# A fused attention and two-MLP kernel: another order of ScalarE's and VectorE's work in the first group, a second block of x through TensorE, and a later first load of r and k

## The chip, the cores and the metric

The kernel runs on one core of a Trainium2 chip. The metric is device time in microseconds (us) of one execution. An execution counts as faster or slower here only from about half a per cent on.

## The reference

Three layers follow each other, all in float32.

```
# 1. linear attention with decay: B=2, H=8 heads, S=768 steps, D=48
y[t]  = r[t] . (state + (u*k[t]) v[t]^T)      # per head
state = w[t] * state + k[t] v[t]^T
# 2. x = y with the heads side by side, [2, 768, 384]
xk = mu_k*x + (1-mu_k)*x_prev ;  xr = mu_r*x + (1-mu_r)*x_prev
x  = sigmoid(xr @ w_r) * (relu(xk @ w_k)**2 @ w_v)          # d_ff = 1024
# 3. gated MLP with a product over the sequence
h = gelu(x @ w_in) ; u, v = halves of h ; v = layernorm(v)*g
out = x + (u * (w_sg @ v + b_sg)) @ w_out
```

## The kernel before, in words

**Units.** The 2 x 768 tokens are cut into 4 groups of 384, and each group's 8 heads into 4 pairs: 16 units, numbered 0 to 15, of one pair over 384 tokens (3 chunks of 128). Units 0 to 3 are the first group. A unit's chunks are worked in parallel form: VectorE first makes decayed copies of r and k (`attn_prep`: two scans `pf` and `pr`, a reciprocal between them, then `kp`, `rp`, `ruk`). TensorE then works a unit in four steps:

- S (`attn_sc`): transposes `kp` into PSUM (`kt_ps`), which ScalarE evicts to `kt`; products of `rp` with `kp` (`sc`), which VectorE masks into `am`; column sums of `ruk`, which VectorE multiplies into `vb`.
- K (`attn_kv`): `kt` by v gives each chunk's state addition `kv`; VectorE adds them up into `zt` and `zcar`, and ScalarE writes scaled copies (`sblk`, `scar`) onto block diagonals. For the first group these ScalarE copies are kept in lists and issued later: "soon" (chunks 0 and 1, four copies a unit) and "late" (the last chunk: `zcar` and two `scar` copies).
- Y (`attn_y`): `am` by v and `vb`, into the PSUM tile `y`.
- Z (`attn_z`): adds `rp` by the scaled states; ScalarE evicts `y` to `yo`, and DMAs carry `yo` into `xx`, which holds x transposed: 3 blocks of 128 rows. A pair has 96 rows, so block 0 takes pairs 0 and 1, block 1 pairs 1 and 2, block 2 pairs 2 and 3.

**Order around the change.** TensorE's order is written out by hand: S0 K0 S1 K1 Y0 Z0 S2 K2 Y1 Z1 S3 K3 Y2 Z2 Y3 Z3, then the first tiles of the second layer (`k`, `r`, `v` steps), between which the next group's units are put. `dummy(n)` issues n matmuls whose result nobody reads: 22 at the start, 2 ahead of each S and Y of the first group, 6 ahead of the first `k` step. Between `in_order.__enter__` and `__exit__`, ScalarE and VectorE run compute instructions strictly in the order in which the program text issues them; elsewhere, and on SyncE's queue of DMAs, priorities set by `at(...)` (planned due times) decide. In that fixed order a unit's "soon" copies stood ahead of the next unit's eviction `kt`.

**The join.** The first `k` step needs all three blocks of `xk` (`moe1_prep`: ScalarE writes `mu*x` to `dx`, VectorE adds `(1-mu)*x_prev` into `xkh`). Blocks 0 and 1 are read from `xx` once its DMAs have landed. Block 2 doesn't wait for a DMA: `sel_run` gathers its rows from the `yo` tiles of pairs 2 and 3 by two matmuls with selection matrices (`sel_make`) into a PSUM bank `bs`, from which ScalarE and VectorE read. Weights come as 64-bit words and are cut to float32 by one ScalarE and one VectorE instruction for each tile (`conv_moe1`: `top`, then `wk`, `wr`, `wv`).

**Queues.** `load_t(0)` issues unit 0's r and k (`urk`) from ScalarE's queue, ahead of `actw`, a one-element sigmoid that brings the activation table in; nearly all other loads, and the DMAs out of `yo`, go through SyncE's queue in order.

Of the kernel before, what the change touches and what calls it, by code (L numbers as in the profile page):

```python
# [17 lines left out]
CH = 128  # L18
# [15 lines left out]
SPARE = 2  # L34
ND0 = 22
ND = 2
ND4 = 4
NDK = 4
N_EARLY = 10
# [28 lines left out]
def emit(tc, tin, nin, vt, consts, ucp, pars, b_sg, w_k, w_v, w_r, w_in, w_sgT, w_out, outT):  # L68
# [22 lines left out]
    class at:  # L91
# [7 lines left out]
        def __exit__(self, *a):  # L99
            tc.cur_priority = self.old  # L100

    subs = []
    for g in range(NG):
# [115 lines left out]
    def wide(i):  # L219
        return i >= NP * N_DIAG  # L220

    def load_uvt(i):
        src = tin[subs[i // NP][0] * NP + i % NP]
        for q in rows(i == NP * N_DIAG):
            with at(TS["Y", i] - 9):
                SP.dma_start(uvts[q], src[q, WL + 2 * G:WL + 3 * G])

    def load_t(i):
        s, hp = divmod(i, NP)
        g, c0, n = subs[s]  # L230
        src = tin[g * NP + hp]
        w, rk = uws[i % 3], urks[i % 3]
        e = A if i < 1 else SP
        for q in rows(i < 3):
            with at(TS["S", i] - 9 if i >= 2 else -19.9 + 0.05 * i):
                SP.dma_start(w[q], src[q, 0:WL])
        for q in rows(i < 3):
            with at(TS["S", i] - 8.5 if i >= 2 else -19.8 + 0.1 * i):
                e.dma_start(rk[q], src[q, WL:WL + 2 * G].rearrange("p (q t) -> p q t", q=2))
        if i == NP * N_DIAG:  # L240
            load_uvt(i)
        uw[i], urk[i] = w, rk

    def load_n(i):
        s, hp = divmod(i, NP)
        g, c0, m = subs[s]
        src = nin[g * NP + hp]
        e = SP if i < 2 else A
        v = pa.tile([128, m, PW], F32, name="uv", tag="uv", bufs=4)
        with at(TS["K", i] - 9 if i >= 2 else -19.5 + 0.1 * i):  # L250
            e.dma_start(v, src[:, c0:c0 + m])
        uv[i] = v
# [133 lines left out]
    def attn_prep(i):  # L386
# [14 lines left out]
        with at(tS - L_PREP):  # L401
            V.tensor_tensor_scan(pf[:, 0:n1], w[:, 0:n1], d1f[:, 0:n1], 1.0, ALU.mult, ALU.max)  # L402
            pe = dr[:, 1:1 + n1].rearrange("p (c t) -> p c t", t=CH + 1)[:, :, CH:CH + 1]
            V.reciprocal(pe, pf3[:, :, CH:CH + 1])
            V.tensor_tensor_scan(pr[:, 1:wl][:, ::-1], w[:, 1:wl][:, ::-1], dr[:, 1:wl][:, ::-1], 0.0, ALU.mult, ALU.add)  # L405
        yield
# [64 lines left out]
    def attn_kv(i):  # L471
# [18 lines left out]
        for c in range(nk):  # L490
# [9 lines left out]
            def scaled(c=c, o=o, sb=sb):  # L500
# [3 lines left out]
                with at(tY - 0.5 + (3 if c == nc_ - 1 else 0.2 * c)):  # L504
                    for h in range(2):
                        hs = slice(h * HP, h * HP + D)
                        A.activation(sb[hs, hs], o[hs], AF.Copy, scale=s["pe"][c][hs])  # L507

# [22 lines left out]
    def attn_z(i):  # L531
# [6 lines left out]
        for c in cs:  # L538
            PE.matmul(y3[0:PR, c], s["us"][c], s["rp"][:, c], start=False, stop=(c == cs[-1]), skip_group_check=True)  # L539
        yo = pa.tile([PR, nc_ * CH], F32, name="yo", tag="yo", bufs=2)  # L540
        s["yo"] = yo
# [7 lines left out]
        with at(TE["Z", i] - 0.2):  # L549
            for h in range(2):  # L550
                a = hp * PW + h * D
                e = a + D
                while a < e:
# [4 lines left out]
                    a += n  # L558
        for f in s.pop("late", []) if i < NP - 1 else []:
            f()  # L560
# [24 lines left out]
    m1 = {}  # L585
    head = {}

    def sel_make():
        t = pl["w"].tile([128, G], F32, name="rs", tag="rs", bufs=3)
        sel = [t[0:PR, q * 128:(q + 1) * 128] for q in range(2)]  # L590
        PL.memset(t, 0.0)
        head["sel"] = sel
        A.activation(sel[0][HP:PR, 0:32], ident[HP:PR, HP + 16:PR], AF.Copy)
        A.activation(sel[1][0:D, 32:32 + D], ident[0:D, 0:D], AF.Copy)
        A.activation(sel[1][HP:PR, 32 + D:128], ident[HP:PR, HP:PR], AF.Copy)

    def sel_run(q):
        x = head["bs"][0]
        if q == 0:
            V.memset(x[:, 0:1], 0.0)  # L600
        PE.matmul(x[:, 1:1 + G], head["sel"][q], st[NP - 2 + q]["yo"], start=(q == 0), stop=(q == 1))

    def moe1_prep(s, which, hold=(), mix=None):
# [8 lines left out]
        def one(j):  # L612
            d = pl["w"].tile([128, t1 - t0], F32, name="dx", tag="dx", bufs=2)
            xj = head["bs"][0] if mix is not None and j == KM - 1 else x[:, j]
            with at(dl - 2.5 + 0.5 * j):
# [277 lines left out]
    with at(-19.95):  # L893
        A.activation(actw, actw, AF.Sigmoid)
    load_t(0)
# [33 lines left out]
    for n, key in enumerate(keys[:n_in]):  # L929
        kd, g = key[0], key[1]  # L930
        if kd in "SY" and g < NP:
            dummy(ND)
        if key == ("Z", NP - 1):
            mix = []
            moe1_prep(0, 0, mix=mix)
            mix[0]()
        if key == ("k", 0, 0):
            mix[1]()
            conv_moe1(0, 1)
            dummy(ND)  # L940
            sel_run(0)
            sel_run(1)
            dummy(NDK)
            rest = attn_prep(NP)
            next(rest)
            mix[2]()
            next(rest)
            conv_moe1(1, 2)
            next(rest, None)
            conv_moe1(2, 3)  # L950
            for f in st[NP - 1].pop("late"):
                f()
            head["order"].__exit__()
        run(key)
        if kd == "K" and g == 0 or kd == "Z" and g < NP - 1:
            for f in st[g + (kd == "Z")].pop("soon"):
                f()
        if kd == "K" and g < NP - 2:
            prep(g + 2)
        if key == ("K", NP - 2):  # L960
            load_unit(NP + 1)
        if kd == "S" and g == NP:
            prep(NP + 1)
            conv_moe1(3)
# [97 lines left out]
```

## Time and profile before

| | us |
|---|---|
| median of 3 runs (lowest, highest) | 364.93 (363.58, 365.13) |
| the profiled execution, its own time | 363.64 |
| its span in the trace | 361.6 |
| TensorE (PE) busy | 343.8 |
| VectorE (DVE) busy | 237.3 |
| ScalarE (ACT) busy | 180.5 |

The span leaves out 2.04 us of the profiled execution's time, before the first and behind the last instruction. Busy time is a sum over the whole span; TensorE's idle time lies almost all in the first 40 us and the last 6. In the timelines below, a line gives the start, the duration (of all instructions merged into it, first start to last end), engine, line of the kernel, operation, out<-in, shapes, count, and in brackets the idle time before it and what ended that.

### The profile page before, as it was taken

To read this page: it belongs to the slowest core of one execution; us is meant where nothing else is said; L and a number is where in the kernel's file an instruction comes from. 1 tells how busy PE (TensorE), PEld (TensorE's weight loads), DVE (VectorE), ACT (ScalarE), POOL (GpSimd) and SP (SyncE) were. 2 spreads that over 40 slices of the span, in tenths; PEclk is the share of its full clock that TensorE was granted. 3 is DMA by queue.
4 is the path that set the end of the run, shared out by engine and by line. 5 is a ranking of instruction groups with operands and counts; after the bars stand their busy time and mean duration, and the time that the engine had idled before them with its cause. 6 is when DMAs were issued, how large, how long until landed. Compare 5 with 4: busy or idle time off the path is not lost.

```text
span 361.6 us, 5957 instructions
## 1 busy us (share of the span) xinstructions
PE 343.8 (95%) x2169; PEld 290.4 (80%) x2169; DVE 237.3 (66%) x515; ACT 180.5 (50%) x427; POOL 41.1 (11%) x64
## 2 busy tenths in 40 slices
PE   8888699989999999999999999999999999999993
PEld 3576367657655568988889999999899998999993
DVE  5972599965548897669643955169889960835531
ACT  2236479766347675167744797395571315301100
POOL 2000003021093200000001316100000000000000
PEclk9899699999999999999999999999999999999999
DMA  8944862655800454001101441451332001010012
GB/s 225 293 161 146 213 188 76 216 146 119 234 3 18 114 152 118 19 16 34 35 18 60 127 134 49 120 177 41 84 78 69 0 22 46 22 45 0 0 70 73
DMA packets 23750, 33.97 MB, mean 94 GB/s; under 512 B 3504, under 2 KB 18032, under 8 KB 23712
## 3 DMA queue, kind: packets, MB, share of 16 engines
q1 hardware_dynamic: 21504, 31.02, 30.3%
q10 hardware_dynamic: 2208, 2.48, 2.5%
q8 instruction: 19, 0.31, 0.4%
q14 instruction: 19, 0.16, 0.2%
HBM read 28.77 MB, written 2.36 MB: 86 GB/s over the span
## 4 chain that ended last, share of the span: by engine, by line
PE 74%; DVE 11%; ACT 6%; DMA 5%; issue 2%; ACTq 0%; SPq 0%; DVEq 0%
PE mm L583 36%; PE mn L583 26%; PE y L525 3%; ACT sblk L507 2%; PE y L539 2%; DMA stg<-w_v 2%; DVE pf L402 2%; PE sc L445 1%; DVE am L468 1%; DMA uw<-tin 1%; PE kv L484 1%; DMA xx<-yo 1%; DVE pr L405 1%; PE mm L909 1%; DVE kl L664 1%
## 5 line engine op out<-in xcount | busy, mean ns | idle before, releaser
L583 PE MATMUL mm<-xkh,wk 128*128 128x384 f32 x96 | 34.6, 506 | 0.0
L571 ACT ACTIVATE gah<-gt 128x384 fp32r<-128x384 f32 x16 | 8.4, 526 | 44.2 <-DVE gt L759 44.2
L583 PEld LDWEIGHTS mm<-xkh,wk 128*128 128x128 f32 x96 | 18.1, 195 | 12.3 <-issue 1.6
L616 ACT ACTIVATE dx<-xx,par 128x384 f32<-128x384 f32 x23 | 14.0, 611 | 26.9 <-DMA xx<-yo 24.7
L507 ACT ACTIVATE sblk<-zt,pf 48x48 f32<-48x48 f32 x64 | 21.2, 331 | 9.3 <-DVE zt L494 6.5
L402 DVE TENSOR_TENSOR_SCAN pf<-uw,d1f 112x387 f32<-112x387 f32 x16 | 16.2, 1011 | 11.3 <-ACT sblk L507 5.0
L583 PE MATMUL mm<-kh,wh 128*128 128x384 f32 x64 | 22.1, 345 | 0.0
L664 DVE TENSOR_TENSOR kl<-kr,kh 128x384 fp32r<-128x384 f32 x24 | 15.1, 629 | 10.2 <-ACT kr L663 10.2
L583 PE MATMUL mm<-kh,wvl 128*128 128x384 f32 x64 | 21.6, 337 | 0.0
L583 PE MATMUL mm<-kl,wh 128*128 128x384 f32 x64 | 21.6, 337 | 0.0
L583 PE MATMUL mn<-wsh,vl 128*128 128x384 f32 x60 | 20.0, 334 | 0.0
L583 PE MATMUL mn<-wsh,vh 128*128 128x384 f32 x60 | 20.0, 334 | 0.0
L583 PE MATMUL mn<-wsl,vh 128*128 128x384 f32 x60 | 20.0, 334 | 0.0
L302 POOL TENSOR_TENSOR w2l<-wf,w2h 128x384 fp32r<-128x384 f32 x12 | 12.8, 1077 | 62.9 <-ACT w2h L301 62.9
L649 ACT ACTIVATE kr<-mm 128x384 f32<-128x384 f32 x27 | 13.0, 480 | 11.5 <-PE mm L583 9.6
L525 PE MATMUL y<-am,uv 128*48 128x128 f32 (+1 forms) x192 | 16.5, 288 | 1.9 <-DVE am L468 1.8
L445 PEld LDWEIGHTS sc<-rp,kp 48*128 48x128 f32 x192 | 12.2, 187 | 6.2 <-issue 4.5
L295 ACT ACTIVATE top<-stg 128x384 f16<-128x384 bf16 x21 | 13.0, 640 | 8.4 <-DMA stg<-w_in 3.9
L468 DVE TENSOR_TENSOR am<-sc,cst 128x384 f32<-128x384 f32 x32 | 16.2, 548 | 1.2 <-PE sc L445 1.2
L583 PE MATMUL mm<-kh,wv 128*128 128x384 f32 x48 | 16.3, 490 | 0.0
L445 PE MATMUL sc<-rp,kp 48*128 48x128 f32 x192 | 15.5, 289 | 0.9 <-DVE am L468 0.9
L405 DVE TENSOR_TENSOR_SCAN pr<-uw,d1r 112x387 f32<-112x387 f32 x16 | 16.0, 998 | 0.4
(210 smaller groups left out, 968.6 us busy)
## 6 DMA issues: line engine op xcount, KB each, us to landing
urk<-tin SPq DMA_DIRECT2D x26, 144.0 KB, 3.3
wh<-w_k SPq DMA_DIRECT2D x8, 384.0 KB, 5.1
stg<-w_v SPq DMA_DIRECT2D x8, 384.0 KB, 4.1
stg<-w_in SPq DMA_DIRECT2D x8, 384.0 KB, 3.5
wq<-tin SPq DMA_DIRECT2D x16, 168.0 KB, 2.5
wsf<-w_sgT SPq DMA_DIRECT2D x12, 192.0 KB, 4.1
outT<-ot SPq DMA_DIRECT2D x12, 192.0 KB, 1.9
uv<-nin ACTq DMA_DIRECT2D x14, 144.0 KB, 2.4
```

The costliest lines, as they stand in the source:

```text
L295: A.activation(box(top.bitcast(F16).rearrange("p (f w) -> p f w", w=2)[:, :, 1]), end, AF.Copy)
L302: e.tensor_tensor(lo, full, hi.bitcast(F32), ALU.subtract)
L402: V.tensor_tensor_scan(pf[:, 0:n1], w[:, 0:n1], d1f[:, 0:n1], 1.0, ALU.mult, ALU.max)
L405: V.tensor_tensor_scan(pr[:, 1:wl][:, ::-1], w[:, 1:wl][:, ::-1], dr[:, 1:wl][:, ::-1], 0.0, ALU.mult, ALU.add)
L445: PE.matmul(sc[h][:, c], s["kp"][hs, c], s["rp"][hs, c], start=True, stop=True)
L468: V.tensor_tensor(am[:, h], sc[h], mask, ALU.mult)
L507: A.activation(sb[hs, hs], o[hs], AF.Copy, scale=s["pe"][c][hs])
L525: PE.matmul(y3[hs, c], uv[i][:, c, h * D:PW if h else HP], s["at"][:, h, c], start=(c == 0), stop=False, skip_group_check=True)
L583: PE.matmul(ps, l, r, start=(first and k == 0), stop=(last and k == len(prods) - 1))
L616: A.activation(d, xj[:, 1 + t0:1 + t1], AF.Copy, scale=mu[:, j:j + 1])
L649: m1[s, "ev", f] = A.activation(kr, ps, AF.Relu).ins
L664: V.tensor_tensor(kl, kr, kh.bitcast(F32), ALU.subtract)
```

## The change

In the first group, a unit's "soon" copies are issued after the next unit's S instead of before it, so that ScalarE evicts `kt` first. For unit 3 they go to VectorE (`tensor_scalar`), issued after K3. Unit 2's "late" copies move behind the join. Block 1 of x is gathered by selection matmuls as block 2 was: four selection matrices, four `sel_run` calls, into both `bs` banks, the first one after Z2, and unit 1's `yo` gets a tile of its own to outlive it; block 0 is mixed ahead of Z2. Unit 4's `attn_prep` is cut once more, and its first scan and the reciprocal are issued ahead of the second block's mix, the second scan behind the third's. The dummy matmuls change from 22 to 20 at the start, from 2 to 4 ahead of each S, from 2 to 1 ahead of each Y of the first group, and from 6 to none ahead of the first `k` step. Unit 0's r and k, and the v tiles of units 2 and 3, are issued on ScalarE's queue behind `actw`.

```diff
@@ -32,10 +34,10 @@
 NTOK = B * S
 NW1 = 2 * KF + KM
 SPARE = 2
-ND0 = 22
-ND = 2
+ND0 = 20
+ND = 1
+NDS = 4
 ND4 = 4
-NDK = 4
 N_EARLY = 10
 T_EARLY = 13.0
 D_EARLY = 1.5
@@ -99,6 +101,7 @@
         def __exit__(self, *a):
             tc.cur_priority = self.old
 
+    head = {}
     subs = []
     for g in range(NG):
         c0 = 0
@@ -219,6 +222,9 @@
     def wide(i):
         return i >= NP * N_DIAG
 
+    def after_table(on):
+        return tc.issue_after(head["actw"]) if on else contextlib.nullcontext()
+
     def load_uvt(i):
         src = tin[subs[i // NP][0] * NP + i % NP]
         for q in rows(i == NP * N_DIAG):
@@ -235,7 +241,7 @@
             with at(TS["S", i] - 9 if i >= 2 else -19.9 + 0.05 * i):
                 SP.dma_start(w[q], src[q, 0:WL])
         for q in rows(i < 3):
-            with at(TS["S", i] - 8.5 if i >= 2 else -19.8 + 0.1 * i):
+            with at(TS["S", i] - 8.5 if i >= 2 else -19.8 + 0.1 * i), after_table(i in (0,)):
                 e.dma_start(rk[q], src[q, WL:WL + 2 * G].rearrange("p (q t) -> p q t", q=2))
         if i == NP * N_DIAG:
             load_uvt(i)
@@ -247,7 +253,7 @@
         src = nin[g * NP + hp]
         e = SP if i < 2 else A
         v = pa.tile([128, m, PW], F32, name="uv", tag="uv", bufs=4)
-        with at(TS["K", i] - 9 if i >= 2 else -19.5 + 0.1 * i):
+        with at(TS["K", i] - 9 if i >= 2 else -19.5 + 0.1 * i), after_table(i in (2, 3)):
             e.dma_start(v, src[:, c0:c0 + m])
         uv[i] = v
 
@@ -402,6 +408,8 @@
             V.tensor_tensor_scan(pf[:, 0:n1], w[:, 0:n1], d1f[:, 0:n1], 1.0, ALU.mult, ALU.max)
             pe = dr[:, 1:1 + n1].rearrange("p (c t) -> p c t", t=CH + 1)[:, :, CH:CH + 1]
             V.reciprocal(pe, pf3[:, :, CH:CH + 1])
+        yield
+        with at(tS - L_PREP):
             V.tensor_tensor_scan(pr[:, 1:wl][:, ::-1], w[:, 1:wl][:, ::-1], dr[:, 1:wl][:, ::-1], 0.0, ALU.mult, ALU.add)
         yield
         pr3 = pr[:, 2:2 + n1].rearrange("p (c t) -> p c t", t=CH + 1)
@@ -504,7 +512,10 @@
                 with at(tY - 0.5 + (3 if c == nc_ - 1 else 0.2 * c)):
                     for h in range(2):
                         hs = slice(h * HP, h * HP + D)
-                        A.activation(sb[hs, hs], o[hs], AF.Copy, scale=s["pe"][c][hs])
+                        if i == NP - 1 and c < nc_ - 1:
+                            V.tensor_scalar(sb[hs, hs], o[hs], s["pe"][c][hs], None, ALU.mult)
+                        else:
+                            A.activation(sb[hs, hs], o[hs], AF.Copy, scale=s["pe"][c][hs])
 
             if i < NP:
                 s.setdefault("late" if c == nc_ - 1 else "soon", []).append(scaled)
@@ -537,7 +548,10 @@
         cs = [c for c in range(nc_) if s["us"][c] is not None]
         for c in cs:
             PE.matmul(y3[0:PR, c], s["us"][c], s["rp"][:, c], start=False, stop=(c == cs[-1]), skip_group_check=True)
-        yo = pa.tile([PR, nc_ * CH], F32, name="yo", tag="yo", bufs=2)
+        if i == 1:
+            yo = pl["w"].tile([128, G], F32, name="kl", tag="kl", bufs=KF)[0:PR]
+        else:
+            yo = pa.tile([PR, nc_ * CH], F32, name="yo", tag="yo", bufs=2)
         s["yo"] = yo
         if hp == 0 and g % GB == 0 and c0 == 0:
             PL.memset(xx[g][:, :, 0:1], 0.0)
@@ -556,7 +570,7 @@
                     q = h * HP + a - hp * PW - h * D
                     (A if i == NP - 1 and h else SP).dma_start(xx[g][p:p + n, j, 1 + c0 * CH:1 + (c0 + nc_) * CH], yo[q:q + n])
                     a += n
-        for f in s.pop("late", []) if i < NP - 1 else []:
+        for f in s.pop("late", []) if i < NP - 2 else []:
             f()
         if hp == NP - 1 and c0 + nc_ == CG and g % GB != GB - 1:
             with at(TE["Z", i] + 2):
@@ -583,22 +597,24 @@
             PE.matmul(ps, l, r, start=(first and k == 0), stop=(last and k == len(prods) - 1))
 
     m1 = {}
-    head = {}
 
     def sel_make():
-        t = pl["w"].tile([128, G], F32, name="rs", tag="rs", bufs=3)
-        sel = [t[0:PR, q * 128:(q + 1) * 128] for q in range(2)]
-        PL.memset(t, 0.0)
+        t = [pl["w"].tile([128, G], F32, name="kl", tag="kl", bufs=KF) for _ in range(2)]
+        sel = [t[q // 2][0:PR, q % 2 * 128:q % 2 * 128 + 128] for q in range(4)]
+        for x in t:
+            PL.memset(x, 0.0)
         head["sel"] = sel
-        A.activation(sel[0][HP:PR, 0:32], ident[HP:PR, HP + 16:PR], AF.Copy)
-        A.activation(sel[1][0:D, 32:32 + D], ident[0:D, 0:D], AF.Copy)
-        A.activation(sel[1][HP:PR, 32 + D:128], ident[HP:PR, HP:PR], AF.Copy)
+        for q, rows_, to, fr in ((0, slice(32, D), 0, 32), (0, slice(HP, PR), 16, HP), (1, slice(0, D), 64, 0),
+                                 (1, slice(HP, HP + 16), 112, HP), (2, slice(HP, PR), 0, HP + 16),
+                                 (3, slice(0, D), 32, 0), (3, slice(HP, PR), 80, HP)):
+            n = min(rows_.stop, PR) - rows_.start if q != 2 else 32
+            A.activation(sel[q][rows_, to:to + n], ident[rows_, fr:fr + n], AF.Copy)
+
+    def sel_bank(j):
+        return head["bs"][j % 2]
 
     def sel_run(q):
-        x = head["bs"][0]
-        if q == 0:
-            V.memset(x[:, 0:1], 0.0)
-        PE.matmul(x[:, 1:1 + G], head["sel"][q], st[NP - 2 + q]["yo"], start=(q == 0), stop=(q == 1))
+        PE.matmul(sel_bank(1 + q // 2)[:, 1:1 + G], head["sel"][q], st[1 + (q + 1) // 2]["yo"], start=(q % 2 == 0), stop=(q % 2 == 1))
 
     def moe1_prep(s, which, hold=(), mix=None):
         g, c0, n = subs[s]
@@ -611,7 +627,7 @@
         dl = TS[("k", "r")[which], s, 0] - (4 if s == 0 and which == 0 else 0)
         def one(j):
             d = pl["w"].tile([128, t1 - t0], F32, name="dx", tag="dx", bufs=2)
-            xj = head["bs"][0] if mix is not None and j == KM - 1 else x[:, j]
+            xj = sel_bank(j) if mix is not None and j else x[:, j]
             with at(dl - 2.5 + 0.5 * j):
                 A.activation(d, xj[:, 1 + t0:1 + t1], AF.Copy, scale=mu[:, j:j + 1])
             with at(dl - 2 + 0.5 * j):
@@ -891,7 +907,7 @@
         mmp["q"] = None
 
     with at(-19.95):
-        A.activation(actw, actw, AF.Sigmoid)
+        head["actw"] = A.activation(actw, actw, AF.Sigmoid).ins
     load_t(0)
     load_t(1)
     with at(-19.75):
@@ -929,36 +945,44 @@
     for n, key in enumerate(keys[:n_in]):
         kd, g = key[0], key[1]
         if kd in "SY" and g < NP:
-            dummy(ND)
-        if key == ("Z", NP - 1):
+            dummy(NDS if kd == "S" else ND)
+        if key == ("Z", NP - 2):
             mix = []
             moe1_prep(0, 0, mix=mix)
             mix[0]()
         if key == ("k", 0, 0):
-            mix[1]()
-            conv_moe1(0, 1)
-            dummy(ND)
-            sel_run(0)
-            sel_run(1)
-            dummy(NDK)
             rest = attn_prep(NP)
             next(rest)
+            sel_run(1)
+            sel_run(2)
+            mix[1]()
+            conv_moe1(1, 2)
+            sel_run(3)
             mix[2]()
             next(rest)
-            conv_moe1(1, 2)
+            next(rest)
+            conv_moe1(2, 3)
             next(rest, None)
-            conv_moe1(2, 3)
-            for f in st[NP - 1].pop("late"):
-                f()
+            for i in (NP - 2, NP - 1):
+                for f in st[i].pop("late"):
+                    f()
             head["order"].__exit__()
         run(key)
-        if kd == "K" and g == 0 or kd == "Z" and g < NP - 1:
-            for f in st[g + (kd == "Z")].pop("soon"):
+        if key == ("Z", NP - 2):
+            conv_moe1(0, 1)
+            sel_run(0)
+        if kd == "S" and 0 < g < NP:
+            for f in st[g - 1].pop("soon"):
                 f()
         if kd == "K" and g < NP - 2:
             prep(g + 2)
         if key == ("K", NP - 2):
             load_unit(NP + 1)
+        if key == ("K", NP - 1):
+            for f in st[g].pop("soon"):
+                f()
+            for q in range(2):
+                V.memset(head["bs"][q][:, 0:1], 0.0)
         if kd == "S" and g == NP:
             prep(NP + 1)
             conv_moe1(3)
```

## Rows read from the trace of the kernel before

**Rows 1.** Stretches, TensorE: stretch, its length, busy us (instructions), clock, DMA share, GB/s
```profile
40.31:46.60 6.29, 6.29 (x12) 0.50 0.80 220
46.60:66.00 19.40, 19.40 (x130) 1.00 0.45 127
...
130.00:355.50 225.50, 224.74 (x1373) 1.00 0.22 62
```

**Rows 2.** Timeline of ScalarE, 6 to 48 us
```profile
14.03 1.40 ACT L507 ACTIVATE sblk<-zt,pf 48x48 f32<-48x48 f32 x4 [4.25 <-DVE zt L494]
15.46 0.45 ACT L434 ACTIVATE kt<-kt_ps 128x336 f32<-128x336 f32 x1
...
20.64 0.49 ACT L548 ACTIVATE yo<-y 112x384 f32<-112x384 f32 x1 [4.73 <-PE y L539]
...
37.34 0.60 ACTq L557 DMA_DIRECT2D xx<-yo  x1
38.37 0.61 ACT L616 ACTIVATE dx<-xx,par 128x384 f32<-128x384 f32 x1 [1.05 <-issue]
```

**Rows 3.** Timeline of TensorE, 8 to 50 us
```profile
15.96 0.88 PE L484 MATMUL kv<-uv,kt 128*64 128x48 f32 x12 [0.70 <-ACT kt L434]
...
20.44 0.59 PE L909 MATMUL mm<-d1f 112*128 112x512 bf16 x2
20.87 0.45 PE L423 MATMUL kt_ps<-cst,kp 112*128 112x112 f32 x3
...
23.86 0.55 PE L484 MATMUL kv<-uv,kt 128*64 128x48 f32 x12 [0.92 <-ACT kt L434]
...
26.33 0.69 PE L539 MATMUL y<-rp,sblk 112*112 112x128 f32 x4
...
32.77 0.69 PE L539 MATMUL y<-rp,sblk 112*112 112x128 f32 x4
...
40.31 2.90 PE L601 MATMUL mm<-yo,rs 112*128 112x384 f32 x4 [3.10 <-DVE mm L600]
...
44.71 4.95 PE L583 MATMUL mm<-xkh,wk 128*128 128x384 f32 x12
```

**Rows 4.** Timeline of VectorE, 5 to 71 us
```profile
14.51 0.96 DVE L402 TENSOR_TENSOR_SCAN pf<-uw,d1f 112x387 f32<-112x387 f32 x1
...
18.19 1.01 DVE L468 TENSOR_TENSOR am<-sc,cst 128x384 f32<-128x384 f32 x2
...
21.95 0.96 DVE L402 TENSOR_TENSOR_SCAN pf<-uw,d1f 112x387 f32<-112x387 f32 x1 [1.67 <-ACT scar L507]
...
47.27 0.96 DVE L402 TENSOR_TENSOR_SCAN pf<-uw,d1f 112x387 f32<-112x387 f32 x1
...
64.54 1.01 DVE L468 TENSOR_TENSOR am<-sc,cst 128x384 f32<-128x384 f32 x2
```

**Rows 5.** Timeline of TensorE, the second layer's start
```profile
51.33 4.14 PE L583 MATMUL mm<-xkh,wk 128*128 128x384 f32 x12
...
65.90 0.88 PE L525 MATMUL y<-am,uv 128*48 128x128 f32 x12
```

**Rows 6.** Stretches, VectorE, the same columns
```profile
47.35:65.50 18.15, 17.29 (x34) 1.00 0.45 121
```

**Rows 7.** Timeline of all engines, 0 to 20 us
```profile
0.73 0.43 ACTq L239 DMA_DIRECT2D urk<-tin  x1
...
1.19 1.28 ACT L894 ACT_TABLE_LOAD   x1 [1.19 <-PEq L1054]
...
2.48 0.20 ACT L894 ACTIVATE actw<-actw 1x1 f32<-1x1 f32 x1
...
7.35 0.56 DVE L409 TENSOR_TENSOR kp<-urk,pr 112x384 f32<-112x384 f32 x1
```

**Rows 8.** Timeline of SyncE's DMA issues, 0 to 80 us
```profile
37.96 1.00 SPq L236 DMA_DIRECT2D uw<-tin  x2
```

**Rows 9.** DMA issues of the first 8 us: KB each, median us to landing
```profile
urk<-tin ACTq DMA_DIRECT2D x1, 336.0 KB, 4.7
```

More of the change, by code (lines that the diff above doesn't have):

```diff
@@ L1 @@
+import contextlib
 import concourse.bass as bass
```

## The prediction

> **What bounds the kernel now.** I read the page's share of each engine first, then the stretches, the timelines of the first 70 us, and the waits. The stretches [rows 1] show two regimes. From 46.6 us on TensorE is busy without a gap at the full clock, and again from 130 to 355.5 us (224.74 of 225.5): there only the time at which its stream starts can move the end. Ahead of 46.6 us it isn't the bound. It stands still for 3.10 us ahead of the selection matmuls at 40.31 [rows 3] and then runs 6.29 us at clock 0.50, the 1.2 GHz level [rows 1]. The reader should see there that what ends last is a chain over engines, unit by unit: in unit 1, ScalarE's four "soon" copies stand from 14.03 ahead of the eviction `kt` at 15.46 [rows 2], and TensorE's K1 waits 0.70 us for that eviction; K2 waits 0.92 us in the same way [rows 3]. The delay comes round: `yo` at 20.64 comes late [rows 2], the "late" copies behind it too, and VectorE's scan `pf` of unit 3 waits 1.67 us for them [rows 4]. At the join, block 1's `dx` at 38.37 sits behind a DMA issue on ScalarE's queue and the landing of `xx` [rows 2].
>
> But the second layer's start has a second, nearly full engine: VectorE is busy 17.29 of 18.15 us from 47.35 to 65.50 [rows 6], its mask for unit 5 starts at 64.54 [rows 4] and TensorE takes it up at 65.90 [rows 5], some 0.35 us after it ends. So I follow two clocks, how much earlier TensorE comes to `k`, and how much earlier VectorE comes to the same work, and the smaller of the two counts.
>
> **The first group, unit by unit.** *Eviction first.* In unit 1 K1 can start 0.70 us earlier, at 15.26, when its predecessors on TensorE end. The two more dummies ahead of S1 cost 0.43 us (two dummies, 20.44 to 20.87 [rows 3]), hidden under the wait of S1's products for VectorE's mask. K1 to Z1 in unit 2's rows takes 26.33 - 23.86 = 2.47 us [rows 3], less 0.2 for one dummy fewer; so Z0 starts at about 17.5. The cost of being wrong here: before, unit 1's steps took longer, 15.96 to 20.64 (`yo`, which waits for Z0's end [rows 2]) less 0.69 for Z0: 3.99, so the same steps at that pace would put Z0 1.5 later. From `yo` to the end of the "late" copies goes 21.95 - 20.64 = 1.31 us [rows 2, 4], so they end near 19.5, and `pf` of unit 3 starts as soon as VectorE is free, 1.67 us earlier, at 20.28.
>
> *The period.* VectorE needs 18.19 - 14.51 = 3.68 us for one unit's copies and, from 18.19 to 20.28 (21.95 less its wait), 2.09 for masks and sums: 5.77 a unit [rows 4]. TensorE needs, from dummies to K, 23.86 - 20.44 - 0.92 = 2.50, plus 0.43 for two more dummies; K to Z 2.47 less 0.2; Z at most 0.69, part of it under the next dummies: 5.7 to 5.9. Before, the period was 32.77 - 26.33 = 6.44 [rows 3]. With 5.8, Z2 starts at 17.5 + 2 x 5.8 = 29.1 instead of 32.77.
>
> *To the last yo.* A selection matmul in float32 is two passes of 384 columns; twelve such passes took 4.14 us [rows 5], so one matmul costs 0.69. Z2 0.5 (its tail under what follows), first selection 0.69, one dummy and Y3 1.7 (2.47 less K's 0.55 and a dummy's 0.2 [rows 3]), Z3 0.69: unit 3's `yo` starts at 32.6 or 32.7 and ends at 33.1 (0.49 [rows 2]). Before, its DMA issue followed it at 37.34: 4.2 us earlier. The four copies that move to VectorE cost 0.35 each on ScalarE (1.40 for four [rows 2]); on VectorE I bound them by 0.2 and 0.35 and take 0.25: 1 us, behind sums of unit 3 that end near 28.2 (two of VectorE's periods of 5.77 from 14.51, masks and sums 2.09), so ready at 29.2 against a need at 31.9. If that cover went, Z3 would slip by at most 1.4. Deferring unit 2's "late" copies takes their 0.8 us out from ahead of `dx`; what is late next is TensorE itself.
>
> **The join.** Before, from the issue at 37.34 to the first `k` at 44.71 went 7.4 us. After, three selections behind Z3 (2.1) end at 34.5; block 1's `dx` waits only for the issue of the DMA on ScalarE's own queue (0.60 plus the 0.43 seen behind it [rows 2]), at 34.1; then `dx` 0.61, `xkh` as long, `top` 0.6, the third `dx` 0.6 and its `xkh` 0.6: all three blocks stand at 36.5. The first `k` starts at 34.5, its third part at 36.5, and its second tile ends at 36.5 + 0.69 + 2.07 = 39.3. Before, these twelve passes ended at 44.71 + 4.95 = 49.66 [rows 3]. TensorE is 10.3 us ahead: 4.2 from the group, the rest from the idle 3.1, the low clock and the six dummies. Should the clock still be low there, the twelve passes cost 0.8 more as before (4.95 against 4.14 [rows 3, 5]), and the three selections up to 2.3 (2.90 for two [rows 3], 1.45 each against 0.69).
>
> **VectorE.** Behind the third `xkh` at 36.5 it has unit 4's second scan (1.0) and five instructions of about 0.5 (17.29 / 34 [rows 6]) to unit 5's `pf`: 39.9 to 40.0, where it was 47.27 [rows 4]. Ahead by 7.3. It cannot close more than the 0.86 us of idle in the next 18.15 us [rows 6]: between 7.3 and 8.2 at unit 5's mask, against TensorE's 10.3. I take 7.8, the middle. TensorE will then wait there for about 2.5 us, which it did not before; from there on both run as before, and beyond 130 us nothing but TensorE.
>
> **The start.** The issue of unit 0's r and k moves from 0.73 [rows 7] to behind the table load, which moves up to about 0.75: 0.75 + 1.28 + 0.20 = 2.25. With 4.7 us to landing [rows 9] it is there at 6.95, and `kp` starts at 7.35 [rows 7]: hidden by 0.4. If it lands 6 us after the issue, `kp` is 0.9 late and VectorE, without a break behind it, carries that through; if the scans ahead of it start earlier because the decays no longer share the engines with it, up to 0.5 is won. I take 0 and keep -0.5 to +0.9. The Trainium skill, "ScalarE: Activation LUTs", section *What ACT_TABLE_LOAD costs*, gives about 1283 ns for the load and about 1380 ns more for a drain. Our trace shows the load but no drain: the sigmoid starts at 2.48, 0.01 us behind the load's end [rows 7]. With the drain the issue would be at 3.6 and `kp` 1 us late, an estimate from that page, and the gain 6.8.
>
> At nothing I cost: more selection matrices (ScalarE waits there anyway), two one-column memsets, a tile of its own for one `yo`, v tiles of units 2 and 3 behind the table load (needed from K2 on).
>
> **The sum.** 363.64 (the profiled execution's own time) - 7.8 = 355.8. It lies 1.3 under the median of three runs, 364.93; half of that on top gives 356.5.
>
> **The rivals.**
> *SyncE's queue decides.* The loads of units 5 to 7 and of weights stand behind unit 3's DMAs: unit 5's decays went at 37.96, right behind the issues at 37.34 [rows 2, 8]. They come forward by 4.2, not by 7.8. For it: unit 5's `pf` would want its decays at 40, and from an issue at 33.8 leaves 6 us. Against: 4.7 to landing is usual [rows 9]. Then the gain is 4.2 to 5: 359 to 360.
> *The lead is eaten.* VectorE's order behind the join is planned anew, and waits appear that weren't there; or the eviction at the head of ScalarE's order, which must wait for transposes, holds the copies that Z needs. Against it: the transposes end long before (K1 waits for nothing else [rows 3]). Gain 0 to 1.8: 363.
> *The clock stays low (slower).* One dummy ahead of Y instead of two, and none ahead of `k`: if the granted clock falls to 1.2 GHz at unit 1, as it did in part before, and now stays there up to the first `k`, the 5.8 us of three units grow. K to the end of Z took 20.64 - 15.96 = 4.68 in unit 1 [rows 2, 3] against 26.33 + 0.69 - 23.86 = 3.16 in unit 2, half as much again: 2.9 a unit, 8.7 in three, and 2.3 for three selections: 7.8 - 8.7 - 2.3, so 3 us slower, 367. It decides from the point where more than two units run low. Against it: dummies a unit rise from 4 to 5, and the idle stretch of 3.1 us is gone.
>
> **How the numbers follow.** My forecast has 0.62, with 353 to 359 as its own range (10.3 ahead kept in full at the one end; 0.9 late at the start, the copies' 1.4 and the low clock's 0.8 at the other: 7.8 - 3.1 = 4.7). SyncE's queue has 0.18, the eaten lead 0.12, the low clock 0.08. For 8 in 10 the range goes from 353 to 361. Half a per cent is 1.8 us, about what can be told from no change: faster 0.82, the same 0.10, slower 0.08.
>
> **What would show it.** Right: `kt` of unit 1 on ScalarE at 12.7, ahead of the copies; `pf` of unit 3 at 20.3 without a wait; Z2 near 29; four selections between 29 and 35; the first `k` near 34.5; clock 1.00 through 34 to 47; a wait of some 2 us of TensorE for VectorE's mask about unit 5's Y. Wrong: a wait of `kp` for its load at the start, unit 5's `pf` waiting for a DMA, a clock of 0.50 behind 16 us, or a first `k` later than 38.

## The result, and the profile after

| | before | after |
|---|---|---|
| median (lowest, highest), us | 364.37 (363.58, 365.13) | 353.24 (352.92, 353.79) |
| the profiled execution, us | 363.64 | 353.79 |
| its span, us | 361.6 | 351.7 |
| TensorE (PE) busy, us | 343.8 | 340.8 |

Four executions of each; the ratio is 0.9696, with a 95% interval of 0.9668 to 0.9724. The medians differ by 11.1 us, the profiled executions by 9.85: before's lay 0.73 us under its median, the changed kernel's 0.55 over its own.

The stretches of all engines after (stretch, length, then busy us and instructions of PE, PEld, DVE, ACT and POOL, granted clock, DMA share, GB/s) stand beside those of [rows 1]. The reader should see the clock column: 1.00 throughout, where before had 0.50 at the join. From 9.0 to 28.9 us TensorE has no gap.

```profile
9.00:28.90 19.90, 19.90 (x233) 15.55 (x231) 18.19 (x43) 8.42 (x25) 0.41 (x1) 1.00 0.81 249
28.90:34.00 5.10, 5.10 (x42) 3.58 (x41) 2.59 (x8) 2.06 (x5) 0.00 (x0) 1.00 0.66 159
34.00:38.40 4.40, 4.30 (x13) 2.08 (x12) 3.83 (x7) 4.34 (x13) 0.33 (x1) 1.00 0.86 248
38.40:56.00 17.60, 17.40 (x123) 11.88 (x121) 16.97 (x33) 14.88 (x34) 2.65 (x2) 1.00 0.65 174
```

ScalarE's timeline after answers to [rows 2]: `kt` stands ahead of the four copies in unit 1, and unit 3's `yo` and its DMA issue come 4.1 us earlier (33.22 for 37.34).

```profile
13.76 0.45 ACT L442 ACTIVATE kt<-kt_ps 128x336 f32<-128x336 f32 x1 [2.91 <-PE kt_ps L431]
14.23 1.40 ACT L518 ACTIVATE sblk<-zt,pf 48x48 f32<-48x48 f32 x4
...
32.70 0.49 ACT L562 ACTIVATE yo<-y 112x384 f32<-112x384 f32 x1 [2.12 <-PE y L550]
33.22 0.60 ACTq L571 DMA_DIRECT2D xx<-yo  x1
33.92 0.58 ACT L632 ACTIVATE dx<-mm,par 128x384 f32<-128x384 f32 x1 [0.73 <-PE mm L617]
```

TensorE's timeline after, beside [rows 3, 5]: S0 at 9.90 (8.84 before), K1 without a wait, Z0 and Z2, the join without a gap, unit 5's Y, and two new waits at unit 5's Z.

```profile
9.90 0.45 PE L431 MATMUL kt_ps<-cst,kp 112*128 112x112 f32 x3
...
15.28 0.55 PE L492 MATMUL kv<-uv,kt 128*64 128x48 f32 x12
...
17.53 0.69 PE L550 MATMUL y<-rp,sblk 112*112 112x128 f32 x4
...
28.84 0.69 PE L550 MATMUL y<-rp,sblk 112*112 112x128 f32 x4
...
32.44 2.10 PE L617 MATMUL mm<-yo,kl 112*128 112x384 f32 x6
34.38 4.67 PE L597 MATMUL mm<-xkh,wk 128*128 128x384 f32 x12
38.89 0.45 PE L431 MATMUL kt_ps<-cst,kp 112*128 112x112 f32 x3
...
55.74 1.21 PE L536 MATMUL y<-am,uv 128*64 128x128 f32 x11 [0.20 <-DVE am L476]
...
60.47 0.47 PE L550 MATMUL y<-rp,sblk 112*112 112x128 f32 x2 [0.40 <-ACT sblk L518]
61.50 0.47 PE L550 MATMUL y<-rp,sblk 112*112 112x128 f32 x2 [0.56 <-ACT sblk L518]
61.81 0.45 PE L431 MATMUL kt_ps<-cst,kp 112*128 112x112 f32 x3
```

How far TensorE is ahead of the kernel before at the same work: 10.61 us at unit 4's S (49.50 to 38.89), 10.16 at unit 5's Y, 9.01 at unit 6's S (70.82 to 61.81, behind the two new waits), 10.35 at unit 6's Y, 9.9 at the end. What it regains at unit 6 is a wait that only the kernel before had:

```profile
78.27 1.21 PE L525 MATMUL y<-am,uv 128*64 128x128 f32 x11 [1.12 <-DVE am L468]
```

VectorE's timeline after, beside [rows 4]. `pf` of unit 5 is 6.95 us earlier (47.27 to 40.32), but the mask `am` of unit 5 is 9.40 us earlier (64.54 to 55.14). Unit 7's scan `pf` and its `ru` now stand behind that mask, and unit 5's sums `zt` behind them:

```profile
40.32 0.96 DVE L408 TENSOR_TENSOR_SCAN pf<-uw,d1f 112x387 f32<-112x387 f32 x1
...
55.14 1.01 DVE L476 TENSOR_TENSOR am<-sc,cst 128x384 f32<-128x384 f32 x2
...
57.54 0.95 DVE L408 TENSOR_TENSOR_SCAN pf<-uw,d1f 112x387 f32<-112x387 f32 x1
58.41 0.59 DVE L422 SCALAR_TENSOR_TENSOR ru<-urk,cst 112x384 f32<-112x384 f32 x1
...
59.45 0.25 DVE L504 SCALAR_TENSOR_TENSOR zt<-zcar,kv 112x48 f32<-112x48 f32 x1
...
60.50 0.23 DVE L504 SCALAR_TENSOR_TENSOR zt<-zt,pf,kv 112x48 f32<-112x48 f32 x1
```

In VectorE's timeline of the kernel before the same two instructions stood ahead of the mask at 64.54:

```profile
62.80 0.95 DVE L402 TENSOR_TENSOR_SCAN pf<-uw,d1f 112x387 f32<-112x387 f32 x1
63.67 0.59 DVE L414 SCALAR_TENSOR_TENSOR ru<-urk,cst 112x384 f32<-112x384 f32 x1
```

The start after, from the timelines of all engines and of VectorE, beside [rows 7]. The issue of r and k moved only from 0.73 to 0.89 and lies beside the table load, not behind it; the table load itself moved from 1.19 to 0.73. The decays that VectorE's first scan waits for came 1.05 us earlier than before (4.09 for 5.14).

```profile
0.73 1.28 ACT L910 ACT_TABLE_LOAD   x1 [0.73 <-PEq L1078]
...
0.89 0.40 ACTq L245 DMA_DIRECT2D urk<-tin  x1
...
2.02 0.20 ACT L910 ACTIVATE actw<-actw 1x1 f32<-1x1 f32 x1
```
```profile
4.09 0.96 DVE L408 TENSOR_TENSOR_SCAN pf<-uw,d1f 112x387 f32<-112x387 f32 x1 [2.37 <-DMA uw<-tin]
...
6.29 0.56 DVE L417 TENSOR_TENSOR kp<-urk,pr 112x384 f32<-112x384 f32 x1
```

### The profile page after: what moved, and what is told of

The parts are those of the page before. It is cut to its first block, busy times and chain, and to the rows that moved or that the text cites. A ratio compares the mean times of both kernels' runs of the same rounds, so it can differ in the third digit from the quotient of the medians.

```text
span 351.7 us, 5968 instructions
## 1 busy us (share of the span) xinstructions
PE 340.8 (97%) x2169; PEld 288.8 (82%) x2169; DVE 239.2 (68%) x520; ACT 180.0 (51%) x427; POOL 41.4 (12%) x65
## 4 chain that ended last, share of the span: by engine, by line
PE 78%; DVE 8%; ACT 8%; DMA 3%; issue 2%; ACTq 0%; DVEq 0%; SPq 0%
PE mm L597 35%; PE mn L597 27%; PE mm L925 3%; PE sc L453 2%; PE y L536 2%; PE y L550 2%; ACT sblk L518 2%; ACT top L301 2%; DMA stg<-w_v 2%; PE kv L492 1%; DVE am L476 1%; DMA urk<-tin 1%; DVE pf L408 1%; ACT wh L307 1%; DVE kl L680 1%
## 5 line engine op out<-in xcount | busy, mean ns | idle before, releaser
L597 PEld LDWEIGHTS mm<-xkh,wk 128*128 128x128 f32 x96 | 17.3, 189 | 12.5 <-DVE xkh L634 1.3
L518 ACT ACTIVATE sblk<-zt,pf 48x48 f32<-48x48 f32 x60 | 19.8, 331 | 5.3 <-DVE zt L502 2.3
L680 DVE TENSOR_TENSOR kl<-kr,kh 128x384 fp32r<-128x384 f32 x24 | 15.1, 629 | 10.3 <-ACT kr L679 10.3
L634 DVE SCALAR_TENSOR_TENSOR dx<-xx,par,dx 128x384 f32<-128x384 f32 x15 | 11.1, 748 | 7.3 <-ACT dx L632 7.3
```

Source lines behind the costliest of these rows:

```text
L597: PE.matmul(ps, l, r, start=(first and k == 0), stop=(last and k == len(prods) - 1))
L680: V.tensor_tensor(kl, kr, kh.bitcast(F32), ALU.subtract)
```

## The experiments

The ratios are against the kernel before, run on the same chip (e1 to e4 on one, e5 to e8 on a second, e10 to e13 on a third). Where a time is set against the changed kernel's 353.24, which comes from another set of runs, the ratios are the better guide. "Profile" below means the one profiled execution of a run.

**Copies ahead of the eviction again (e1).** In the changed kernel only the order goes back, unit 3's copies to ScalarE with it:

```diff
-        if kd == "S" and 0 < g < NP:
-            for f in st[g - 1].pop("soon"):
+        if kd == "K" and g == 0 or kd == "Z" and g < NP - 1:
+            for f in st[g + (kd == "Z")].pop("soon"):
                 f()
...
-                        if i == NP - 1 and c < nc_ - 1:
+                        if False:
```

> The changed kernel with one thing undone: the "soon" copies stand ahead of the next unit's eviction again, and unit 3's are back on ScalarE. Theory (the eviction first is worth 4 us, the join the rest): TensorE waits for the eviction again by 0.7 to 0.9 us a unit and for unit 3's copies ahead of Z3; unit 3's yo comes 3 to 4 us later than at 32.7, the first k at 37.5 to 38.5 instead of 34.4, and the time is 356 to 357.5. Rival (the join alone, with the clock kept up, brings the gain; the group has slack ahead of it): within 1 us of the changed kernel, 353 to 354.

Measured: 356.06 us, ratio 0.9758 (0.9728 to 0.9787), 2.8 slower than the changed kernel. The period from one unit's Z to the next rises from 5.65 to 6.2 us, and unit 4's S comes 1.0 later though S0 was 0.58 earlier (9.32). The eviction's order is worth 1.6 there. The rest of the difference between the two profiles is clock: behind the same two waits at unit 5's Z, twelve passes take 5.80 us instead of 4.14. But that is one execution (mean clock 0.991, 356.31 us): three of the other four have a mean clock of 0.998 to 0.999 and still take 355.12 to 356.26, so what costs those the part above 1.6 stays open. TensorE's timeline, then a stretch of it (length, busy, clock, DMA share, GB/s):

```profile
9.32 0.45 PE L431 MATMUL kt_ps<-cst,kp 112*128 112x112 f32 x3
...
39.89 0.45 PE L431 MATMUL kt_ps<-cst,kp 112*128 112x112 f32 x3
...
61.47 0.47 PE L550 MATMUL y<-rp,sblk 112*112 112x128 f32 x2 [0.40 <-ACT sblk L518]
62.50 0.47 PE L550 MATMUL y<-rp,sblk 112*112 112x128 f32 x2 [0.56 <-ACT sblk L518]
...
64.64 5.80 PE L597 MATMUL mm<-xrh,wr 128*128 128x384 f32 x12
```
```profile
64.00:68.00 4.00, 4.00 (x18) 0.58 0.73 253
```

The clock of unit 1 stayed at 1.00, where it fell in the kernel before. So the clock holds there without the eviction's new order too; e10 and e11 ask through which part.

**Block 1 from its DMA again (e2).** `sel_bank` for block 2 only, `sel_run(0)` and `sel_run(1)` gone:

```diff
-            xj = sel_bank(j) if mix is not None and j else x[:, j]
+            xj = sel_bank(j) if mix is not None and j == KM - 1 else x[:, j]
```

> The changed kernel with block 1 of x read from xx after its DMAs again; its two selection matmuls are gone, all else stays in its place. Theory (block 1's selection is a necessary part of the join's gain): block 1's dx waits for the landing, behind unit 2's yo at 30.1 by three issues and some 2 to 4 us, and the first k's second part comes 1 to 2 us later: 354.5 to 355.5. Rival (with unit 2's yo 4 us earlier the DMA lands before ScalarE is free for that dx at 33.9, and the third block, at 36.1, ends last anyway): the same as the changed kernel within 0.5 us, 352.8 to 353.8, two selections' 1.4 us of TensorE saved at no effect.

Measured: 353.67 us, ratio 0.9692 (0.9664 to 0.9721): the same. The first `k` starts at 32.49 and its second tile ends at 37.96. Counted from S0 (9.18 here, 9.90 in the changed kernel) that is 1.2 and 0.4 us earlier, in spite of a wait for the block:

```profile
32.49 0.81 PE L597 MATMUL mm<-xkh,wk 128*128 128x384 f32 x2
34.11 3.85 PE L597 MATMUL mm<-xkh,wk 128*128 128x384 f32 x10 [0.81 <-DVE xkh L634]
```

The lead is lost again at unit 5's Z, which waits 0.49 and 0.70, and in the clock behind it (0.61 over 60 to 64, 0.53 over 64 to 68). All five executions have a mean clock of 0.988 to 0.992, under the changed kernel's 0.995 to 0.999. With the group ended earlier, the second selection buys nothing that the time shows.

**The first load back ahead of the table (e3).** `after_table` returns an empty context:

```diff
-        return tc.issue_after(head["actw"]) if on else contextlib.nullcontext()
+        return contextlib.nullcontext()
```

> The changed kernel with unit 0's r and k, and the v tiles of units 2 and 3, issued ahead of the one-element sigmoid again. Theory A (the later issue freed the engines for the decays: they landed 1.05 us earlier, and it counts): decays land near 5.1 again, VectorE's first scan starts there, the time is 0.5 to 1 us longer, 353.8 to 354.3. Theory B (the landing differs by chance, or TensorE's dummy matmuls, which end at 9.9, hide it): 353.2 within 0.4.

Measured: 353.82 us, ratio 0.9713 (0.9679 to 0.9746): the same. The first scan starts at 4.92 instead of 4.09, but S0 stood behind the dummies at 9.86 in this profile, as at 9.90 in the changed kernel's, so this profile is theory B's; the time, at the lower end of theory A's range and 0.2 over theory B's, doesn't tell the two apart.

**The dummies of before (e4).** 22 at the start, 2 ahead of S and Y, 6 ahead of the first `k`:

```diff
-ND0 = 20
-ND = 1
-NDS = 4
+ND0 = 22
+ND = 2
+NDS = 2
...
+            dummy(2)
             sel_run(1)
...
             sel_run(3)
+            dummy(4)
```

> The changed kernel with the numbers of dummy matmuls of before: 22 at the start, 2 ahead of each S and each Y of the first group, and 2 and 4 about the selections ahead of the first k. Theory (TensorE is without a gap from 9 to 34 us, so each dummy counts by 0.21 us there, but the third block's xkh ends last at the join): two fewer ahead of S1, S2, S3, one more ahead of each of four Y: 0.4 us less in the group; six more at the join cost 1.3 but start under a wait of about 0.8: 0 to +0.5 in all, 353.2 to 353.7. Rival (the four dummies ahead of each S hold the clock up): the granted clock falls to 0.5 in unit 1 or at the join and the time is 1.5 to 4 us longer, 355 to 357.

Measured: 353.06 us, ratio 0.9687 (0.9657 to 0.9718): the same, with the clock at 1.00 (S0 at 9.87). The first `k` is 0.7 later (35.08) and unit 4's S is level (38.95): dummies lie in time in which TensorE would wait.

**The eviction alone, on the kernel before (e5).** The new order of the copies, with unit 3's on VectorE, and nothing else:

```diff
-        if kd == "K" and g == 0 or kd == "Z" and g < NP - 1:
-            for f in st[g + (kd == "Z")].pop("soon"):
+        if kd == "S" and 0 < g < NP:
+            for f in st[g - 1].pop("soon"):
                 f()
+        if key == ("K", NP - 1):
+            for f in st[g].pop("soon"):
+                f()
```

> The kernel before with one part of the change alone: the "soon" copies behind the next unit's S, unit 3's on VectorE. Theory (my prediction's split: 4.2 us of lead from the eviction first, the rest from the join): unit 3's yo ends near 33.5 instead of 37.3, the join stays 7.4 us long at the low clock, and the time is 360 to 361. Rival (undoing it in the changed kernel cost only 1 us up to the second layer, so the eviction is worth about 1 where the clock stays up): 362.5 to 364.

Measured: 356.37 us, ratio 0.983 (0.9795 to 0.9865): a gain of 6.8 where 3 to 4 were expected, a miss. The profile shows why: unit 1 ran at clock 1.00 (0.59 before, over 16 to 20 us), though S0 came only at 10.11, and unit 3's `yo` is 4.7 us earlier; the low clock, which before reached 1.9 us into the first twelve `k` passes (4.95 us), is over when they begin (4.04); and the 1.12 us wait at unit 6's Y is gone (1.3 us of lead won from there on). The idle stretch at the join is still there:

```profile
35.45 2.88 PE L604 MATMUL mm<-yo,rs 112*128 112x384 f32 x4 [2.96 <-DVE mm L603]
...
39.37 4.04 PE L586 MATMUL mm<-xkh,wk 128*128 128x384 f32 x12
```

**The join alone (e6).** The changed kernel with the edits of e1, e3 and e4 together.

> The changed kernel with the "soon" order, the first load and the dummy matmuls of before; what is left of the change is the join: selections for block 1, early memsets and first scan, deferred late copies. Theory (the join brings about 6 of the 10 us): first k at 36 to 38.5, time 357 to 359. Rival (eviction and join each remove the same waits, so that either alone brings most): 354 to 356.

Measured: 359.34 us, ratio 0.9896 (0.986 to 0.9931), just over the 357 to 359 expected. The join's gap is gone, the first `k` comes at 39.68 (36 to 38.5 expected), the clock is 1.00 from there. Unit 1 is as before: Z0 at 19.91, clock 0.57 from 16 to 20 us. The gains of e5 and e6 (6.8 and 3.8) add up to 10.6 of the whole 11.1, yet e1, which takes the eviction out of the whole, loses only 2.8 (and e6 has the first load and the dummies of before besides).

**Which part lifts unit 1's clock (e10, e11).** The edits of e1 and e3 together (e10), and those of e1 and e4 (e11).

> The changed kernel with two parts undone: the copies ahead of the eviction again, and unit 0's r and k issued first again; the new dummies and the selection of block 1 stay. With the copies alone undone Z0 started at 17.28; with copies, load and dummies undone together it started at 19.91, at clock 0.57 between 16 and 20 us. Theory 1, the four dummies ahead of S hold the clock of unit 1: clock 1.00 between 16 and 20, Z0 at 17.2 to 17.6, time as with the copies alone undone, 355.5 to 356.5. Theory 2, the order of the first loads does: clock below 0.7 there, Z0 at 19.5 to 20, 358 to 359.

> The changed kernel with the copies ahead of the eviction again and the dummies as before; the later load and the selection of block 1 stay. Theory 1 (the dummies hold the clock of unit 1): clock near 0.6 between 16 and 20, Z0 at 19.5 to 20, 358 to 359. Theory 2 (the order of the first loads): clock 1.00, Z0 at 17.2 to 17.6, 355.5 to 356.5. If both this run and the one with copies and load undone show 1.00, either is enough, or the clock of unit 1 changes from run to run.

Measured: e10 358.63 us (0.9823, 0.9758 to 0.9888), e11 356.78 (0.9775, 0.971 to 0.9841), three executions each (357.45 to 358.66 and 355.44 to 357.34). e10 is as theory 2 has it; e11's median is 0.28 us over theory 2's range, its profile (355.44) inside. With the copies ahead of the eviction, the clock goes with the load and not with the number of dummies: 1.00 in the profiles with the later load (e1, e11), 0.57 to 0.59 in those with the first (e6, e10). In e10 the first scan starts at 5.03, S1's products wait 0.31 us for VectorE's mask and K1 0.71 for `kt`, and the clock falls; in e11 the scan starts at 3.98, K1 alone waits 0.50, and the clock holds. TensorE of e10, a timeline and a stretch:

```profile
8.87 0.45 PE L431 MATMUL kt_ps<-cst,kp 112*128 112x112 f32 x3
...
12.99 1.40 PE L453 MATMUL sc<-rp,kp 48*128 48x128 f32 x12 [0.31 <-DVE am L476]
...
15.86 0.87 PE L492 MATMUL kv<-uv,kt 128*64 128x48 f32 x12 [0.71 <-ACT kt L442]
...
19.66 0.69 PE L550 MATMUL y<-rp,sblk 112*112 112x128 f32 x4
```
```profile
16.00:20.00 4.00, 4.00 (x40) 0.59 0.52 190
```

The same of e11:

```profile
9.29 0.45 PE L431 MATMUL kt_ps<-cst,kp 112*128 112x112 f32 x3
...
14.81 0.55 PE L492 MATMUL kv<-uv,kt 128*64 128x48 f32 x12 [0.50 <-ACT kt L442]
...
17.28 0.69 PE L550 MATMUL y<-rp,sblk 112*112 112x128 f32 x4
```
```profile
16.00:20.00 4.00, 4.00 (x50) 1.00 0.60 207
```

So with r and k issued later, and the decays earlier for it, unit 1 stays off the low clock, which is worth 2.4 us at Z0. (e10's profile lost clock once more later, 0.69 over 68 to 72 us, so its time isn't all unit 1's.)

But S0 differs too, 8.87 in e10 and 9.29 in e11, and over all 14 profiles that differs as much as the decays do. The table counts S0 from VectorE's first scan:

| profiles | first scan, us | S0, us | S0 behind the scan, us | wait of S1's products for the mask, us | unit 1's clock |
|---|---|---|---|---|---|
| before, e6, e10 | 5.03 to 5.14 | 8.84 to 9.01 | 3.70 to 3.96 | 0.31 to 0.89 | falls (0.57 to 0.59) |
| e13 (below) | 4.00 | 7.29 | 3.29 | 0.90 | falls (0.50) |
| e3, e5 | 4.92, 4.96 | 9.86, 10.11 | 4.94, 5.15 | none | 1.00 |
| the other eight, e1 and e11 among them | 3.94 to 4.21 | 8.82 to 9.90 | 4.88 to 5.82 | none | 1.00 |

Where S0 follows the scan closely, TensorE waits for VectorE in unit 1 and its clock falls; where it doesn't, the clock holds (no profile lies between 3.96 and 4.88). The eviction's order doesn't sort them: e1 and e11 hold without it, e13 falls with it. e3 and e5, with the eviction first and the load of before, held at an S0 that came late, although 24 dummies stood ahead of it as in before, e6 and e10. So that the eviction alone keeps the clock isn't shown; no run had it with the load of before and an early S0.

**Unit 7's scan behind unit 5's sums (e7).** In `attn_prep`, with `zt1` the instruction of unit 5's second sum:

```diff
-        with at(tS - L_PREP):
+        with at(tS - L_PREP), (tc.issue_after(st[i - 2]["zt1"]) if i == 7 else contextlib.nullcontext()):
             V.tensor_tensor_scan(pf[:, 0:n1], ...
```

> The changed kernel with one more edge: VectorE issues unit 7's first scan only behind unit 5's state sums, which stood behind it and six more instructions. Theory (TensorE's new wait of 0.96 us ahead of unit 5's Z, for ScalarE's copies of sums that VectorE makes 4 us after K5, is what remains of the lead's loss): the wait falls under 0.4 us, and the end comes 0.5 to 1.2 us earlier, 352 to 352.7. Rival (the lead lost there comes back at unit 6's mask anyway, for which TensorE waited before): 353 to 353.5.

Measured: 352.56 us, ratio 0.9717 (0.9684 to 0.9751). The waits at unit 5's Z are gone:

```profile
58.80 0.92 PE L552 MATMUL y<-rp,sblk 112*112 112x128 f32 x4
```

Counted from S0 (8.82 here, 9.90 in the changed kernel), unit 6's S is 1.2 us earlier. Of that 0.6 goes again in waits for unit 6's mask. The time is inside the theory's range, but by the ratio (0.9717 against 0.9696) it isn't faster than the changed kernel, which wasn't run on this chip.

**The same with block 1 from its DMA (e8).** The edits of e7 and e2.

> Both: block 1 of x from the DMA (two selection matmuls fewer), and unit 5's sums ahead of unit 7's scan. Theory: the second layer starts a good microsecond earlier, as with the DMA alone, and without the long wait ahead of unit 5's Z the clock stays at 2.4 GHz in the r steps (with the DMA alone it fell to 0.5 from 61 to 67 us, which cost 1.7 there): 351.3 to 352.3, faster than the changed kernel. Rival (VectorE is full, and a start that is a microsecond earlier only makes the waits longer): 353 to 354.

Measured: 352.40 us, ratio 0.9716 (0.9683 to 0.9748), clock 1.00 from 60 to 72: level with e7, a little over the theory's range, and not shown to be faster than the changed kernel.

**The changed kernel again (e12), and e8 with fewer dummies (e13).** Six executions each, on one chip. Against e8, e13 has:

```diff
-ND0 = 20
-ND = 1
-NDS = 4
+ND0 = 16
+ND = 1
+NDS = 2
```

> The changed kernel itself once more, for comparison on the same chip with the version that has unit 7's first scan behind unit 5's sums, block 1 from its DMA and fewer dummies: 353.2, between 352.9 and 353.8; first k near 34.4, S4 near 38.9, TensorE waiting 0.4 and 0.56 us for ScalarE's copies ahead of Z5.

> The changed kernel with unit 7's first scan behind unit 5's sums and block 1 from its DMA (two selection matmuls fewer), and now also 16 dummies at the start instead of 20 and 2 ahead of each S instead of 4. If the dummies at the start are what S0 waits for, S0 comes up to 0.9 earlier, at 9.0 to 9.9, and the time is 351.0 to 352.0, 1.2 to 2 under the changed kernel. If the clock needs them, it falls in units 0 to 3 (below 0.8 between 9 and 30), Z0 comes at 18 or later and the time is 353 or more. If neither, 352.4 as with 20 and 4.

Measured: e12 353.31 us (352.82 to 354.38; ratio 0.9691, 0.9642 to 0.974), the expected time, with the two waits at unit 5's Z (0.41 and 0.55). S0 came at 9.00 in this profile, and the first `k` and unit 4's S 0.9 us earlier than expected (33.47, 37.99). TensorE of e12:

```profile
9.00 0.45 PE L431 MATMUL kt_ps<-cst,kp 112*128 112x112 f32 x3
...
33.47 4.68 PE L597 MATMUL mm<-xkh,wk 128*128 128x384 f32 x12
```

e13 354.46 (351.95 to 355.55; 0.9701, 0.9644 to 0.9758). With fewer dummies S0 comes at 7.29, ahead of what VectorE has ready; S1's products wait 0.90 for its mask and the clock falls to 0.50. TensorE of e13, a timeline and a stretch:

```profile
11.97 2.11 PE L453 MATMUL sc<-rp,kp 48*128 48x128 f32 x12 [0.90 <-DVE am L476]
```
```profile
12.00:16.00 4.00, 4.00 (x30) 0.50 1.02 339
```

Four of its six executions have a mean clock of 0.980 to 0.987 and take 354.4 to 355.6; the two at 0.998 and 0.999 take 352.0. No version tried beats the changed kernel by more than a measurement can tell.

## Why the prediction was right

The forecast's range, 353 to 361, held the 353.24, but only by 0.24 us, and the forecast itself, 356.5, was 3.3 too long. The range's lower end stands for TensorE's 10.3 us kept in full; by the prediction's own sum that end is 363.64 - 10.3 = 353.3, or 354.0 with the half of 1.3 that it adds elsewhere, so that 353.24 lies inside is in part luck. Up to the first `k` the mechanism was the one forecast; what it said would then bound the gain, VectorE, did not. The gain was 2 us larger than its sum (9.85 against 7.8 of the profiled executions).

- *Eviction first, the period, the last yo.* K1 at 15.28 (15.26 forecast), Z0 17.53 (17.5), the period 5.65 (5.8), Z2 28.84 (29.1), unit 3's `yo` 32.70 to 33.19 (32.6 to 33.1), the copies on VectorE 1.01 us (1 us). Unit 3's `pf` starts at 19.58 with 0.36 of wait left (20.28 without one). The period and the lengths of the steps were forecast well; that the times agree to a few hundredths is luck. K1's 15.26 was worked out from before's rows, with S0 at 8.84 and the 0.89 us wait of S1's products. In the changed kernel that wait is gone, since the decays came earlier, and S0 came 1.06 later. In its second profile (e12, S0 at 9.00) K1 is at 14.37, Z0 at 16.63 and the first `k` at 33.47, all some 0.9 ahead of the forecast; `kt` of unit 1 is at 12.85 there (12.7 forecast) and at 13.76 in the first. And the step gave all of unit 1's gain to the eviction, where the table under e11 has it with S0's distance from VectorE's first scan.
- *The join.* First `k` 34.38 (34.5), third `xkh` ends 36.15 (36.5), the second tile ends 39.05 (39.3): 10.6 us ahead (10.3; 11.5 in e12). Right in time, but e2 came to the same time without the second selection.
- *VectorE: the term that was mis-sized.* The prediction gave VectorE 7.3 us at unit 5's `pf` and said that it "cannot close more than the 0.86 us of idle" up to the mask, so 7.8, with TensorE waiting some 2.5 us. Measured: 6.95 at `pf`, 9.40 at the mask, a wait of 0.20. From `pf` to the mask went 14.82 us instead of 17.27. The failed step took the instructions between the two as fixed. Behind the join the planner orders VectorE: unit 7's `pf` and `ru` went behind the mask (1.38 us with their gaps, 62.80 to 64.18), one `wk` ahead of `pf` (about 0.5); the rest, some 0.6, is less idle time (0.5) and shorter `xrh` (0.8), less a longer `kp` (0.8), and small differences. So VectorE's 7.8 did not set the end: TensorE's lead was 10.61 at unit 4's S, 9.01 at its lowest, and 9.9 at the end.
- *What was late next.* TensorE paid 0.96 us at unit 5's Z (0.23 before), a place that the prediction didn't name. The new order, with unit 5's sums behind unit 7's scan, is part of it: the second sum starts 5.36 us behind the mask instead of 4.90. The larger part is that TensorE had come 0.76 nearer to VectorE by then (10.16 ahead against 9.40). The rival in which the lead is eaten by a new order was right in kind; its price was at most 1 us, not 6 to 8.
- *The start.* Taken at 0 with -0.5 to +0.9. The premise was wrong: the issue went out beside the table load, at 0.89 and not at 2.25, and `kp` never waits for it. It came with decays that landed a microsecond earlier (0.5 at most was allowed for), which the dummies ahead of S0 hide, and which counts through unit 1's clock where S0 would otherwise follow the scan too closely (e10 against e11). In the changed kernel's first profile S0 came 1.06 us later than before's; with S0 at 9.00 (e12) the span is 350.9 instead of 351.7. That can account for the 0.55 us by which the profiled execution lay over its median; the other 0.73 between 9.85 and the medians' 11.1 comes from the kernel before, whose profiled execution lay that much under its median.
- *SyncE's queue, the low clock.* Neither rival came true: unit 5's `pf` waits for no DMA, and the clock is 1.00 from 9.0 to 56 us.

Open: what the new order at unit 5's mask is worth by itself (unit 7's scan ahead of the mask, as before, wasn't run); and how much of unit 1's clock is due to the eviction alone, for the reason given under e11.

## What to carry to other kernels

A second engine bounds the start only as far as its order is fixed: where a planner sets it, list what stands ahead of the instruction in question, and ask which of it another engine needs later and the planner may move. When two edits may remove the same stall, undo them in pairs: undone alone, each can look cheap. Before an engine's clock is put down to an edit, compare its start with that of the engine that feeds it in every profile at hand. Filler matmuls that lie in a wait cost nothing (e4), and taking them out can cost more than they do (e13).

## What the runs showed of the hardware

- A DMA issue that the program puts behind an activation on ScalarE went out at 0.89 us, while the table load that this activation brings ran from 0.73 to 2.01 and ahead of the activation itself at 2.02.
- With the issue of r and k 0.16 us later (0.89 for 0.73), that of a v tile 0.05 later and the table load 0.46 earlier, the decays, issued at 0.73 in both, landed about 1 us earlier: the first scan started at 3.94 to 4.21 in the nine profiles with that order and at 4.92 to 5.14 in the five without it (before, e3, e5, e6, e10). Which of the three moves does it wasn't separated.
- The same two waits, 0.40 and 0.56 us in front of unit 5's Z, left the clock at 1.00 in the changed kernel (0.41 and 0.55 in its second profile, 1.00 too) and were followed by 0.58 in e1. The waits alone don't decide; what else does wasn't found.
- The last 15 dummies ahead of S0 took 4.47 us in one profile of the changed kernel and 3.56 in the other (S0 at 9.90 and 9.00), the same instructions from the same 5.60 us. Over the 13 profiles with 24 dummies ahead of it, S0 came between 8.82 and 10.11.
- In the kernel before, the mean granted clock of an execution went with its time: on one chip 366.4 and 366.6 us at 0.975, 362.1 and 362.3 at 0.989. The changed kernel lay at 0.995 to 0.999 in all ten executions, and there it doesn't order the times: 354.38 and 352.82 both at 0.999.
